# Four pairs' q and k rows set side by side by GpSimd and transposed as 96x128; the output's transposing DMA put ahead of q's and k's

## Chip, core and metric

One core of a Trainium2 chip runs the whole program. The metric is the device time of one execution in microseconds (us), and the kernel is compared with itself before the change. The profile of one execution gives the durations used below.

## What is computed

Attention with a bias that depends on the distance of two positions alone, and behind it two matrix products with a leaky ReLU between them:

```python
scores = (1 / np.sqrt(D)) * np.matmul(q, k.transpose(0, 1, 3, 2))   # B, H, S, D = 8, 8, 576, 64
scores = scores + bias_table[bucket].transpose(2, 0, 1)[None]       # bucket: from |i - j|
attn = softmax(scores)                                              # over the last axis
x = np.matmul(attn, v).transpose(0, 2, 1, 3).reshape(B * S, H * D)  # 4608 x 512
h = x @ w_in                                                        # 512 x 2048
return np.maximum(0.01 * h, h) @ w_out                              # 2048 x 512
```

## The kernel before

**Pairs and bodies.** The heads of a batch are taken two by two: pair `n` is batch `n // 4`, heads `2p` and `2p + 1` with `p = n % 4`, and there are 32 pairs, 0 to 31. Body `n` of the main loop computes the scores of pair `n` (`score`, `qk_mm`, `exp`), multiplies the probabilities of pair `n - 1` with v (`av_tails`, `av` or `av_phase`, `divide`), and makes q and k of pair `n + 1` ready (`transpose_q`, `transpose_k`). From body 4 on, pieces of the two big products fill TensorE in between: `ffn_in` (`pm` from `xT` and `w_in_sb`, L459, its leaky ReLU on ScalarE at L472) and `ffn_out` (L486). From body 8 on, most bodies run in halves of the rows (`body_in_halves`, L407 and L610). The order on each engine is the order in which the program writes the instructions; nothing reorders them.

**q and k.** They are loaded by GpSimd's DMAs with 96 rows on the partitions and six chunks of 64 numbers per head (`qn`, `kn`, two buffers by batch). TensorE needs them transposed. For pairs 0 to 8, `turned_pair` makes, for each of q and k, 12 transposes on TensorE (L275): one for each of six chunks and two heads, 96x64 in, 64x96 out, the two heads' outputs one above the other in `ps_t`. VectorE or ScalarE then copies `ps_t` into `qt` (L290) or `kt` (L294). For pairs 9 to 31 (`by_dma`), VectorE sets the rows of the two heads side by side (`pair_rows`, `pr`, L257), one transposing DMA on SyncE turns q and k at once (`turn_by_dma`, `tu`, L265), and the copies read `tu`. `pr` has four buffers.

**The bias.** After the exponential (L325 and others on ScalarE), `band` multiplies parts of the probabilities `at` by a table `hk` on VectorE (L348, both inputs in SBUF); there are five such products per pair.

**The output.** `divide` writes the quotients of pair `n` into `opair` (L381, L383). They are transposed into `xT`, on TensorE with a copy (`ps_tx`, L433 and L434) or, for pairs 6 and 8 to 30 (`x_by_dma`), by a transposing DMA on SyncE (L423). `ffn_in` of the next 512 tokens can start once the last pair of a batch stands in `xT`.

**SyncE's queue.** In a body in halves, SyncE runs two `fence` instructions (L391, each waits for TensorE and releases a later product), then the turning DMA of q and k, then that of the output, then stores of the output.

**GpSimd's queue.** `loads(n)` issues the DMAs of later batches at the start of body `n`: in body 0 the first half of `w_in`, v of batch 1, the second half of `w_in` and the first half of `w_out`; in body 2 half of q and k of batch 2 and the second half of `w_out`; from body 5 on, each behind a copy of one number (`tick`, L772) that waits for `opair`.

**PSUM.** The tag `m` has two banks, taken in turn by `ps_t`, `ps_tx` and the `pm` of the pieces.

Of the kernel before, what the change touches and what calls it, by code (L numbers as in the profile page):

```python
# [37 lines left out]
def kernel(  # L38
# [10 lines left out]
    nc = tc.nc  # L49
# [7 lines left out]
    n_pairs = H // 2  # L57
# [25 lines left out]
    ident = per.tile([P, P], BF16, name="ident")  # L83
# [11 lines left out]
    RQ = 96  # L95
    NC = S // RQ
    qn = [per.tile([P, H, NC, D], BF16, name=f"qn{i}") for i in range(NBUF)]
    kn = [per.tile([P, H, NC, D], BF16, name=f"kn{i}") for i in range(NBUF)]
# [18 lines left out]
    def load_v_part(b, chunks, h0=0, h1=H):  # L117
        for c in chunks:
            nc.gpsimd.dma_start(  # L119
                out=vn[b % NBUF][:, c, h0:h1, 0:D],  # L120
                in_=v[b, h0:h1, c * P : (c + 1) * P, :].rearrange("h s d -> s h d"),
            )
# [56 lines left out]
    for j, (u, lo, w, m) in enumerate(groups):  # L179
        copy = nc.scalar.copy if j % 3 == 2 else nc.vector.tensor_copy  # L180
        copy(out=ub[:, C0 + lo : C0 + lo + m * w].rearrange("h (m w) -> h m w", w=w),
             in_=e8[:, u : u + m].unsqueeze(2).to_broadcast([H, m, w]))
    row = ub[:, :]
    nc.vector.tensor_copy(
        out=ub[:, C0 - BAND + 1 : C0],
        in_=bass.AP(tensor=row.tensor, offset=row.offset + C0 + BAND - 1,
                    ap=[list(row.ap[0]), [-1, BAND - 1]]),
# [45 lines left out]
    def load_w_in(half):  # L233
        o = slice(half * (DF // 2), (half + 1) * (DF // 2))
        nc.gpsimd.dma_start(out=w_in_sb[:, :, o], in_=moe_w_in[:, o].rearrange("(c p) f -> p c f", p=P))

    def load_w_out(half):
        n = n_fc // 2
        nc.gpsimd.dma_start(
            out=w_out_sb[:, half * n : (half + 1) * n, :],  # L240
            in_=moe_w_out[half * n * P : (half + 1) * n * P, :].rearrange("(f p) e -> p f e", p=P),
        )
# [7 lines left out]
    prs, turned = {}, {}  # L250

    def pair_rows(n):

        b, p = items[n]
        t = prs[n] = pr_pool.tile([RQ, 2, NC, 2 * D], BF16, name="pr")
        for j, src in enumerate((qn, kn)):
            nc.vector.tensor_copy(out=t[:, j, :, :].rearrange("r c (e d) -> r c e d", e=2),  # L257
                                  in_=src[b % NBUF][0:RQ, 2 * p : 2 * p + 2, :, :].rearrange("r e c d -> r c e d"))

    def by_dma(n):  # L260
        return n > 2 * n_pairs
# [5 lines left out]
    def turned_pair(n, j):  # L267

        if by_dma(n):
            return turned[n][:, j * NC : (j + 1) * NC, :].rearrange("p c r -> p r c")  # L270
        ps = ps_m_pool.tile([P, 8 * P], BF16, name="ps_t", tag="m")
        b, p = items[n]
        for c in range(NC):
            for e in range(2):
                nc.tensor.transpose(ps[e * D : (e + 1) * D, c * RQ : (c + 1) * RQ],  # L275
                                    in_=(qn, kn)[j][b % NBUF][0:RQ, 2 * p + e, c, :],
                                    identity=ident[0:RQ, 0:RQ])
        return ps[:, 0:S].rearrange("p (c r) -> p r c", c=NC)
# [13 lines left out]
    def transpose_k(n):  # L292
        kt = kts[n] = kts_[n % 2]
        nc.vector.tensor_copy(out=kt[:, 0:S].rearrange("p (r c) -> p r c", c=NC), in_=turned_pair(n, 1))  # L294
        apart(kt)
# [56 lines left out]
    def av_tails(n):  # L352

        b, p = items[n]
        at4 = at4_[n % 2]
        ops_[n] = op_pool.tile([P, NJ + 1, 2 * D], BF16, name="opair")
        ps = outs[n] = [ps_o_pool.tile([P, 512], FP32, name="ps_o", tag=f"o{e}") for e in range(2)]
        for ic in range(NJ + 1):
            for e in range(2):
                r = slice(e * SL, (e + 1) * SL)  # L360
                nc.tensor.matmul(ps[e][:, ic * (D + 1) : (ic + 1) * (D + 1)],  # L361
                                 lhsT=at4[r, ic * P : (ic + 1) * P], rhs=v4[b % NBUF][r, p, :],
                                 start=(ic == 0), stop=False)
# [25 lines left out]
    def fence(sooner):  # L389

        f = nc.sync.nop(nofuse=True)  # L391
        tc.add_manual_dep(f.ins, sooner.ins.name, ended, reason="behind the last products of these rows")
        return f
# [21 lines left out]
    def x_by_dma(n):  # L415
        return n_pairs + 2 <= n < N - 1 and n != 2 * n_pairs - 1

    def x_transposes(n, spare=None):
        b, p = items[n]
        opair = ops_[n]  # L420
        w = (NJ + 1) * P
        if x_by_dma(n):
            nc.sync.dma_start_transpose(  # L423
                out=xT[p][:, b * S : b * S + w].rearrange("p (i t) -> p i t", t=P),
                in_=opair.rearrange("p i d -> p (i d)"),
            )
            return
        if spare is None:
            ps = ps_m_pool.tile([P, 8 * P], BF16, name="ps_tx", tag="m")
        else:  # L430
            ps = ps_o_pool.tile([P, 8 * P], BF16, name="ps_tx", tag=spare)
        for ic in range(NJ + 1):
            nc.tensor.transpose(ps[:, ic * P : (ic + 1) * P], in_=opair[:, ic, :], identity=ident)  # L433
        nc.vector.tensor_copy(out=xT[p][:, b * S : (b + 1) * S], in_=ps[:, 0:S])  # L434
# [194 lines left out]
    def body_in_halves(n, kinds):  # L629

        loads(n)
        turns = rows_ahead(n) if by_dma(n + 1) else []
        score(n, 0)
        av_tails(n - 1)
        last = fence(av_phase(n - 1, 0))
        score(n, 1)
        T, s = made["out"], at_piece["out"]
        if kinds[0] == "out":
            one, two = open_piece("out", (T, s)), open_piece("out", (T, s + 4))
        else:  # L640
            one, two = open_piece("in"), open_piece("out")
        phase = side_by_side(one, two)
        phase(0, 0, 1)
        av_phase(n - 1, 1, last)
        if n + 1 < N:
            transpose_q(n + 1)
        band(n, 0)
        divide(n - 1, range(2))
        last = fence(phase(0, 1, n_cc))
        score(n, 2)  # L650
        score(n, 3)
        phase(1, 0, n_cc, last)
        band(n, 1)
        if n + 1 < N:
            transpose_k(n + 1)
        score(n, 4)
        if kinds[0] == "in":
            one[2]()
        for m in turns:
            turn_by_dma(m)  # L660
        if x_by_dma(n - 1):
            x_transposes(n - 1)
        while stores:
            o, y = stores.pop(0)
            nc.sync.dma_start(out=o, in_=y)
        if not x_by_dma(n - 1):
            late = [n - 1]
        else:
            late = []
        band(n, 2)  # L670
        if kinds[0] == "out":
            outs_pm[T] = one[0]
            ffn_out(T, s + 1)
            band(n, 4)
            score(n, 5)
            band(n, 5)
            ffn_out(T, s + 2)
            ffn_out(T, s + 3)
            for m in late:
                x_transposes(m, "o0")  # L680
                finished(m)
            outs_pm[T] = two[0]
            for part in range(5, 8):
                ffn_out(T, s + part)
            at_piece["out"] = (s + 8) % n_fc
            made["out"] += at_piece["out"] == 0
            return
        piece_out()
        band(n, 4)
        score(n, 5)  # L690
        band(n, 5)
        piece_out()
        piece_out()
        for m in late:
            x_transposes(m, "o1")
            finished(m)
        room["left"] -= 5
        moe(room["left"], 0)
# [59 lines left out]
    def loads(n):  # L758

        b, p = items[n]  # L760
        if n == 0:
            load_w_in(0)
            load_v_part(1, range(NJ))
            load_v_tail(1)
            load_w_in(1)
            load_w_out(0)
        elif n == 2:
            load_qk(2, 0, H // 2)
            load_w_out(1)
        if b < 1 or p < 1 or b > B - 2:  # L770
            return
        nc.gpsimd.tensor_copy(out=tick, in_=ops_[n - 2][0:1, 0, 0:1])  # L772
        if p == 1:
            load_qk(b + 1, H // 2, H)
            load_v_part(b + 1, (0,))
        elif p == 2:
            load_v_part(b + 1, (1, 2, 3))
        else:
            load_v_tail(b + 1)
            if b + 2 < B:  # L780
                load_qk(b + 2, 0, H // 2)
# [6 lines left out]
    def rows_ahead(n):  # L788
        ms = [m for m in range(n + 2, min(n + AHEAD + 1, N))
              if by_dma(m) and m - (AHEAD if m > 2 * n_pairs + 2 else 2) == n]  # L790
        for m in ms:
            pair_rows(m)
        return ms
# [5 lines left out]
    def score(n, u):  # L799
        exp(n, u, qk_mm(n, u))  # L800
# [44 lines left out]
    n = n_pairs  # L845
# [129 lines left out]
```

## Time and profile before

| | |
|---|---|
| time, median of three runs | 377.12 us (376.32 to 378.21) |
| profiled execution | 375.74 us, its span 374.0 us |
| granted TensorE clock, mean | 0.997 |
| TensorE busy | 362.5 us, 97% of the span |
| ScalarE, VectorE, GpSimd busy | 240.8, 196.5 and 77.3 us |

The page gives one execution: busy time of each engine, the chain of work that ended last, and the costliest groups of instructions by source line. The timeline gives instructions in order with their start, duration and the idle time of the engine before them; a run of equal instructions stands in one row with its count. `PE` is TensorE, `PEld` its weight load, `DVE` VectorE, `ACT` ScalarE, `POOL` GpSimd, `SP` SyncE. The end of a product on TensorE is modelled, so its rows overlap, and the distance from one start to the next is the sharper measure.

### The profile page before, as it was taken

The page shows a single profiled execution, that of the slowest core. Times are in us where ns is not written, and L with a number is a line of the kernel's source. Part 1 is how long each engine was busy: PE and PEld are TensorE (multiplying, and loading weights), DVE is VectorE, ACT ScalarE, POOL GpSimd, SP SyncE. Part 2 cuts the span into 40 slices and gives each one's busy share as a digit, 9 for nine tenths or more (in the row PEclk, how much of TensorE's full clock was granted, in tenths as well). Part 3 has the DMA queues.
Part 4 walks back from the last instruction along what each step waited for, and adds up shares of the span by engine and source line. Part 5 has one row for each costly group of instructions (what it writes and reads, how often), then busy time and mean ns, then how long its engine had stood idle before and what let it go on. Part 6 is the DMA issues. An engine that isn't in the chain of part 4 may idle for free.

```text
span 374.0 us, 10606 instructions
## 1 busy us (share of the span) xinstructions
PE 362.5 (97%) x4516; PEld 187.5 (50%) x4516; DVE 196.5 (53%) x504; ACT 240.8 (64%) x374; POOL 77.3 (21%) x118
## 2 busy tenths in 40 slices
PE   7889999999999999999999999999999999999995
PEld 3455555555555555555555554555555544444442
DVE  3688577776757566666755565665554200100121
ACT  4998887568947787777877776777777364054000
POOL 8773331333023303331233023100000000000000
PEclk9999999999999999999999999999999999999998
DMA  8999999799579979996999599433121000200221
GB/s 103 189 201 184 206 201 158 124 166 169 67 107 163 121 124 122 148 140 121 96 121 145 83 115 156 93 80 71 34 43 47 30 28 0 86 28 0 86 79 64
DMA packets 104360, 40.19 MB, mean 107 GB/s; under 512 B 83184, under 2 KB 98808, under 8 KB 104312
## 3 DMA queue, kind: packets, MB, share of 16 engines
q0 software_dynamic: 53696, 18.36, 47.3%
q1 hardware_dynamic: 50472, 21.02, 28.3%
q8 instruction: 35, 0.57, 0.6%
q10 hardware_dynamic: 144, 0.13, 0.1%
q14 instruction: 13, 0.11, 0.1%
HBM read 37.68 MB, written 9.45 MB: 126 GB/s over the span
## 4 chain that ended last, share of the span: by engine, by line
PE 89%; ACT 4%; DVE 4%; DMA 2%; issue 1%; DVEq 0%; ACTq 0%
PE pm L486 28%; PE pm L459 28%; PE pm L610 8%; PE ps_s L312 7%; PE ps_o L407 6%; PE ps_o L372 4%; DMA xT<-opair 2%; ACT at L325 2%; PE ps_s L315 2%; PE ps_o L361 1%; PE ps_w L750 1%; DVE opair L383 1%; PE ps_t L275 1%; PE ps_tx L433 1%; PE ps_q L305 1%; DVE at L348 1%
## 5 line engine op out<-in xcount | busy, mean ns | idle before, releaser
L325 ACT ACTIVATE at<-ps_s 128x1024 bf16<-128x1024 f32 x128 | 124.5, 1027 | 26.1 <-PE ps_s L312 26.0
L472 ACT ACTIVATE gt<-pm 128x512 bf16<-128x512 f32 x138 | 82.8, 605 | 71.0 <-PE pm L459 70.5
L459 PE MATMUL pm<-xT,w_in_sb 128*128 128x512 bf16 x508 | 118.1, 379 | 0.1
L486 PE MATMUL pm<-w_out_sb,gt 128*128 128x512 bf16 x492 | 113.9, 379 | 0.0
L348 DVE TENSOR_TENSOR at<-at,hk 128x768 bf16<-128x768 bf16 (+3 forms) x160 | 71.0, 454 | 59.3 <-ACT at L325 34.8
L459 PEld LDWEIGHTS <-w_in_sb 128*128 128x128 bf16 x508 | 47.6, 98 | 54.8 <-issue 0.7
L486 PEld LDWEIGHTS <-gt 128*128 128x128 bf16 x492 | 45.0, 98 | 51.4
L504 DVE COPY y<-pm 128x512 f32<-128x512 f32 x35 | 24.2, 692 | 74.8 <-PE pm L486 74.8
L312 PE MATMUL ps_s<-qt,kt 64*128 64x512 bf16 x256 | 43.2, 380 | 3.4 <-ACT at L325 3.0
L610 PE MATMUL pm<-w_out_sb,gt 64*128 64x512 bf16 x168 | 42.2, 376 | 0.0
L610 PE MATMUL pm<-xT,w_in_sb 64*128 64x512 bf16 x136 | 37.7, 376 | 0.9 <-DMA xT<-opair 0.9
L772 POOL COPY tick<-opair 1x1 bf16<-1x1 bf16 x18 | 3.9, 215 | 134.8 <-DVE opair L383 134.8
L119 POOL DMA_DIRECT2D vn<-in_v_dram x32 | 29.9, 940 | 8.8 <-DMA w_out_sb<-in_moe_w_out_dram 3.8
L383 DVE TENSOR_TENSOR opair<-ps_o,rcp 128x320 bf16<-128x320 f32 x64 | 29.7, 488 | 1.6
L407 PE MATMUL ps_o<-vn,at 64*128 64x65 bf16 x1520 | 29.5, 190 | 0.0
L407 PEld LDWEIGHTS <-at 64*128 64x128 bf16 x1520 | 27.1, 94 | 4.4 <-SPq L391 3.0
L312 PEld LDWEIGHTS <-kt 64*128 64x128 bf16 x256 | 11.6, 94 | 25.3 <-issue 16.5
L332 ACT ACTIVATE at<-ps_s 128x576 bf16<-128x576 f32 x32 | 21.8, 680 | 0.2 <-PE ps_s L316 0.2
L381 DVE RECIPROCAL rcp<-ps_o 128x5 f32<-128x5 f32 x64 | 10.0, 182 | 22.3 <-PE ps_o L372 19.3
L328 ACT ACTIVATE at<-ps_q 128x256 bf16<-128x256 f32 x64 | 21.3, 394 | 0.3 <-PE ps_q L305 0.2
L372 PE MATMUL ps_o<-vn,at 128*128 128x65 bf16 x520 | 20.1, 194 | 0.0
L372 PEld LDWEIGHTS <-at 128*128 128x128 bf16 x520 | 17.9, 97 | 3.5 <-issue 0.7
(62 smaller groups left out, 244.4 us busy)
## 6 DMA issues: line engine op xcount, KB each, us to landing
out_dram<-y SPq DMA_DIRECT2D x35, 256.0 KB, 2.2
qn<-in_q_dram POOLq DMA_DIRECT2D x14, 288.0 KB, 5.9
kn<-in_k_dram POOLq DMA_DIRECT2D x14, 288.0 KB, 7.5
vn<-in_v_dram POOLq DMA_DIRECT2D x28, 128.0 KB, 6.4
w_in_sb<-in_moe_w_in_dram POOLq DMA_DIRECT2D x2, 1024.0 KB, 12.4
w_out_sb<-in_moe_w_out_dram POOLq DMA_DIRECT2D x2, 1024.0 KB, 15.9
qn<-in_q_dram POOLq DMA_DIRECT2D x4, 144.0 KB, 4.7
kn<-in_k_dram POOLq DMA_DIRECT2D x4, 144.0 KB, 5.0
```

What stands on the lines that cost most here:

```text
L119: nc.gpsimd.dma_start(out=vn[b % NBUF][:, c, h0:h1, 0:D], in_=v[b, h0:h1, c * P : (c + 1) * P, :].rearrange("h s d -> s h d"),)
L312: nc.tensor.matmul(ps[:, e, :], lhsT=kt[r, u * P : (u + 1) * P], rhs=qt[r, 0:512], start=True, stop=True)
L325: nc.scalar.activation(at[:, :, u, 0:512], ps, AF.Exp, scale=scale)
L348: nc.vector.tensor_tensor(out=o, in0=o, in1=m, op=ALU.mult)
L372: nc.tensor.matmul(ps[:, ic, :], lhsT=at[:, o : o + P], rhs=vn[b % NBUF][:, c, 2 * p + e, :], start=False, stop=(ic == NJ and c == NJ - 1))
L383: nc.vector.tensor_tensor(out=opair[:, :, e * D : (e + 1) * D], in0=ps[:, :, 0:D], in1=rcp.to_broadcast([P, NJ + 1, D]), op=ALU.mult)
L407: m = nc.tensor.matmul(outs[n][e][:, ic * (D + 1) : (ic + 1) * (D + 1)], lhsT=at[halves[r], o : o + P], rhs=vn[b % NBUF][halves[r], c, 2 * ...
L459: nc.tensor.matmul(pm, lhsT=w_in_sb[:, c, f * P : (f + 1) * P], rhs=xT[c][:, t0 : t0 + TT], start=(c == 0), stop=(c == n_cc - 1))
L472: nc.scalar.activation(g, pm, AF.Prelu, bias=0.0, scale=1.0, alpha=0.01)
L486: nc.tensor.matmul(pm, lhsT=gt[:, f, ts * P : (ts + 1) * P], rhs=w_out_sb[:, f, :], start=(f == 0), stop=(f == n_fc - 1))
L504: nc.vector.tensor_copy(out=y, in_=pm)
L610: m = nc.tensor.matmul(pm, lhsT=w[halves[r]], rhs=x[halves[r]], start=(k == 0 and c == 0), stop=(low is not None and k == 1 and c == n_cc ...
```

## The change

For pairs 5 to 8, GpSimd copies the two heads' rows side by side into `pr` (k first, then q, 96x768 each), and TensorE transposes both heads of a chunk at once: six transposes 96x128 for each of q and k in place of twelve 96x64. The copies of pairs 5 and 6 stand in GpSimd's queue in body 0, ahead of the first half of `w_out`; those of pair 7 in body 2 behind the second half of `w_out`; those of pair 8 in body 6 behind three loads of v. For the pairs from 9 on, VectorE still makes the copies, now k ahead of q. In bodies in halves the output's transposing DMA is issued ahead of the one of q and k, where it was behind it. Order and number of the instructions of ScalarE, and the number of those of VectorE and SyncE, stay as they are.

```diff
         t = prs[n] = pr_pool.tile([RQ, 2, NC, 2 * D], BF16, name="pr")
-        for j, src in enumerate((qn, kn)):
-            nc.vector.tensor_copy(out=t[:, j, :, :].rearrange("r c (e d) -> r c e d", e=2),
+        eng = nc.vector if by_dma(n) else nc.gpsimd
+        for j, src in reversed(list(enumerate((qn, kn)))):
+            eng.tensor_copy(out=t[:, j, :, :].rearrange("r c (e d) -> r c e d", e=2),
                                   in_=src[b % NBUF][0:RQ, 2 * p : 2 * p + 2, :, :].rearrange("r e c d -> r c e d"))
...
         for c in range(NC):
+            if n > n_pairs:
+                nc.tensor.transpose(ps[:, c * RQ : (c + 1) * RQ], in_=prs[n][:, j, c, :],
+                                    identity=ident[0:RQ, 0:RQ])
+                continue
             for e in range(2):
...
         if kinds[0] == "in":
             one[2]()
+        late = [n - 1]
+        if x_by_dma(n - 1):
+            x_transposes(late.pop())
         for m in turns:
             turn_by_dma(m)
-        if x_by_dma(n - 1):
-            x_transposes(n - 1)
         while stores:
             o, y = stores.pop(0)
             nc.sync.dma_start(out=o, in_=y)
-        if not x_by_dma(n - 1):
-            late = [n - 1]
-        else:
-            late = []
...
             load_w_in(1)
+            pair_rows(n_pairs + 1)
+            pair_rows(n_pairs + 2)
             load_w_out(0)
         elif n == 2:
             load_qk(2, 0, H // 2)
             load_w_out(1)
+            pair_rows(n_pairs + 3)
...
             load_v_part(b + 1, (1, 2, 3))
+            if b == 1:
+                pair_rows(2 * n_pairs)
```

## The prediction

> **What bounds the kernel now.** I read the page first, then a table of busy time by stretch, then TensorE's waits, then the timeline of the bodies that the change touches.
>
> ```profile
> span 374.0 us, 10606 instructions
> PE 362.5 (97%) x4516; PEld 187.5 (50%) x4516; DVE 196.5 (53%) x504; ACT 240.8 (64%) x374; POOL 77.3 (21%) x118
> ```
>
> TensorE is the bound of the whole, but a share over the span hides where it is not. The table by stretch has, for each, its length and then the busy time of PE, PEld, DVE, ACT and POOL. The first row is body 3 and the start of body 4, the next two are bodies 5 and 6, the last holds body 24 and the start of body 25.
>
> ```profile
> 25.00:33.00 8.00, 7.09 (x151) 4.84 (x148) 6.02 (x18) 7.94 (x12) 3.62 (x5) 1.00 1.61 189
> 38.70:47.40 8.70, 8.70 (x120) 5.05 (x120) 5.33 (x13) 7.14 (x11) 2.83 (x5) 1.00 1.25 204
> 47.40:56.10 8.70, 8.70 (x120) 5.04 (x121) 6.45 (x16) 7.15 (x11) 2.59 (x5) 1.00 1.39 200
> 210.00:230.00 20.00, 19.14 (x296) 10.07 (x295) 11.46 (x29) 14.30 (x22) 5.25 (x8) 1.00 0.87 113
> ```
>
> From 25 to 33 us ScalarE is the bound (7.94 of 8.00 busy), with TensorE and VectorE passing work round in a ring. In bodies 5 and 6 TensorE is busy without a break, so what is taken from it there counts, unless it only waited inside its modelled busy time. In the last row TensorE stands still for 0.86 us, and its list of waits (total, times, longest) names why:
>
> ```profile
> PE pm L610 <- DMA xT<-opair: 0.9, 1, 0.9
> ```
>
> **Part 1: the transposes on TensorE.** The change takes 48 products away: four pairs, q and k, six each. These are body 6's rows, then those of the end of body 7.
>
> ```profile
> 48.78 0.45 PE L275 MATMUL ps_t<-ident,qn 96*64 96x96 bf16 x12
> 49.16 1.04 PE L459 MATMUL pm<-xT,w_in_sb 128*128 128x512 bf16 x4
> 50.74 0.45 PE L275 MATMUL ps_t<-ident,kn 96*64 96x96 bf16 x12
> 51.12 0.61 PE L312 MATMUL ps_s<-qt,kt 64*128 64x512 bf16 x4
> ...
> 51.84 0.45 PE L433 MATMUL ps_tx<-ident,opair 128*128 128x128 bf16 x5
> 52.28 1.89 PE L459 MATMUL pm<-xT,w_in_sb 128*128 128x512 bf16 x8
> 54.01 0.38 PE L315 MATMUL ps_s<-qt,kt 128*128 128x512 bf16 x1
> ...
> 54.25 1.89 PE L459 MATMUL pm<-xT,w_in_sb 128*128 128x512 bf16 x8
> 56.08 0.60 PE L312 MATMUL ps_s<-qt,kt 64*128 64x512 bf16 x4
> ...
> 59.42 0.45 PE L275 MATMUL ps_t<-ident,kn 96*64 96x96 bf16 x12
> 59.80 1.04 PE L459 MATMUL pm<-xT,w_in_sb 128*128 128x512 bf16 x4
> ```
>
> From start to start a side's 12 transposes hold TensorE for 0.38 us. There is a second cost in them. Eight L459 products take 1.73 us when a product with the same 128*128 weights follows (52.28 to 54.01), and 1.83 when one with 64*128 weights follows (54.25 to 56.08): a change of the weights' shape costs 0.10. The old transposes (96*64) stand between 128*128 products, so q pays it on the way in, outside the 0.38, and on the way out, inside. New ones are 96*128; I take them to share a shape class with 128*128, as nothing in the table is nearer. Their price comes from the output's transposes in body 4, and the group of those transposes' weight loads (busy us, mean ns):
>
> ```profile
> 33.57 0.45 PE L433 MATMUL ps_tx<-ident,opair 128*128 128x128 bf16 x5
> 33.86 0.38 PE L315 MATMUL ps_s<-qt,kt 128*128 128x512 bf16 x1
> ```
>
> ```profile
> L433 PEld LDWEIGHTS <-opair 128*128 128x128 bf16 x40 | 2.3, 97 | 2.6 <-DVE opair L383 2.2
> ```
>
> Five transposes with 128 weight columns and 128 moving columns take 0.29 us, 58 ns each. Six take 0.35 at that price, or 0.26 if the 96 moving columns scale it. So a q side gains 0.38 + 0.10 less 0.26 to 0.35: 0.13 to 0.22; I take 0.20. Against this speaks a rule of the Trainium skill, TensorE: Matmul & The Clock Gate, section "LDWEIGHTS (loading the stationary operand)": the load takes its columns divided by 1.2 ns, so that twice the columns take twice as long. By it, as an estimate, six loads of 107 ns would hold TensorE for 0.64 us and a side would lose 0.16 where I let it gain 0.20; the 58 ns above, with 128 columns each, do not bear that out for loads in a row.
>
> Not every side counts. On the k sides of bodies 5 and 6 the gain runs into a wait: at 51.84 five transposes take 0.44 where they took 0.29, since the next `pm` needs the bank that VectorE is still emptying of `ps_t`:
>
> ```profile
> 51.48 0.75 DVE L294 COPY kt<-ps_t 128x576 bf16<-128x576 bf16 x1
> ```
>
> It ends at 52.23, and TensorE goes on at 52.28. That copy is behind `divide` on VectorE, released by the end of `av` before the k transposes, so shorter transposes there only lengthen the wait: 0. In body 4 both sides run into waits for VectorE and ScalarE (the q side into the leaky ReLU of the piece before): 0. On the k side of body 7 a 128*128 product follows (59.80) and no such wait is seen: 0.20. Sum: three q sides and one k side, 0.8 us (0.5 to 0.9).
>
> **Part 2: the output's DMA first.** The chain of waits has, before that stop of TensorE:
>
> ```profile
> 215.16 0.89 DVE opair L383 x2
> ...
> 217.13 8.64 DMA xT<-opair
> ```
>
> and SyncE's timeline what it did meanwhile:
>
> ```profile
> 215.59 1.44 SPq L265 DMA_TRANSPOSE tu<-pr  x1
> ```
>
> `opair` is there at 216.05, but SyncE was busy issuing the other DMA until 217.03. First in the queue, the output's goes out 1.1 us earlier, and no transfer of q and k is ahead of it. 1.1 is more than the 0.86 that TensorE lost, so the whole stop goes: 0.86 (0 if the landing does not move with the issue). What is late next is nothing on DMA: the turned q and k, now some 1.9 us later, are read two bodies on, and a body is 8.7 us at its shortest. Behind both in SyncE's queue are stores and the next body's fences, which wait 0.5 us longer at most, with half a body to spare. VectorE's k-ahead-of-q order costs nothing, since one DMA waits for both.
>
> **Part 3: GpSimd's copies.** Eight copies of 96x768. No row has such a copy; the nearest are fills of a constant and of the identity, and the selection that finishes it; VectorE's own copy of that size (group row: busy us, mean ns) stands beside them.
>
> ```profile
> 0.24 0.10 POOL L959 MEMSET const-float32-0.0<- 128x1 f32 x1 [0.24 <-issue]
> 2.69 0.24 POOL masks.py:197 MEMSET ident<- 128x128 bf16 x1
> 3.01 0.29 POOL masks.py:199 TENSOR_SCALAR_AFFINE_SELECT ident<-ident 128x128 bf16<-128x128 bf16 x1
> ```
>
> ```profile
> L257 DVE COPY pr<-kn 96x768 bf16<-96x768 bf16 x23 | 8.1, 350 | 0.0
> ```
>
> From 1 to 128 elements a fill grows by 0.14 us, 1.14 ns per element, so 768 elements take 0.1 + 0.87: about 1.0 us. As ends I keep VectorE's 0.35 and, from the selection's 1.5 ns per element, 1.25. GpSimd's queue around them:
>
> ```profile
> 26.92 0.80 POOL L235 DMA_DIRECT2D w_in_sb<-in_moe_w_in_dram  x1
> 31.72 0.90 POOL L239 DMA_DIRECT2D w_out_sb<-in_moe_w_out_dram  x1 [4.00 <-DMA w_in_sb<-in_moe_w_in_dram]
> ...
> 54.03 0.62 POOL L132 DMA_DIRECT2D v<-in_v_dram  x1 [3.13 <-DMA w_out_sb<-in_moe_w_out_dram]
> ```
>
> Four copies stand in a hole of 4.0 us. Behind them are queued `w_out`, q, k and v of batch 2 and the ticks. Even 2 us of lateness there is covered: issues wait for earlier transfers (the 4.00 and 3.13), and the second `w_out` half, landed by 54, is first read by products behind the last row of body 7 above (59.80). The copies of pairs 5 and 6 end by 33 even if they wait as reckoned below, and pair 6's are read from body 5 on, behind 38.70. If that cover were gone, TensorE would wait microsecond for microsecond.
>
> The price lies on VectorE. A copy of one number on GpSimd shows it:
>
> ```profile
> 36.73 0.65 DVE L348 TENSOR_TENSOR at<-at,hk 128x192 bf16<-128x192 bf16 x2
> 36.90 0.52 POOL L772 COPY tick<-opair 1x1 bf16<-1x1 bf16 x1
> 41.05 0.18 POOL L772 COPY tick<-opair 1x1 bf16<-1x1 bf16 x1 [1.45 <-DVE opair L383]
> ```
>
> It takes 0.18, but 0.52 when a band product runs, and ends 0.04 after that product (37.42 against 37.38): GpSimd waited for VectorE's whole instruction. No row shows the other direction; whatever both need whole, I take to be needed by both alike, so that a band that finds a copy running waits for its end. The Trainium skill, SBUF — State Buffer, section "Who interferes with whom", says so too: a VectorE instruction with two SBUF inputs and a GpSimd one that reads SBUF exclude each other, and the later is blocked until the earlier ends. The trace agrees for the one direction, with the 0.52 us above. The bands beside the copies are, before the change:
>
> ```profile
> 27.94 0.42 DVE L348 TENSOR_TENSOR at<-at,hk 128x512 bf16<-128x512 bf16 x1
> ...
> 28.98 0.55 DVE L348 TENSOR_TENSOR at<-at,hk 128x768 bf16<-128x768 bf16 x1
> ...
> 29.98 1.11 DVE L348 TENSOR_TENSOR at<-at,hk 128x768 bf16<-128x768 bf16 x3
> ```
>
> If copies and bands take turns: the first copy runs from 27.72 to 28.72, the band of 27.94 starts at 28.72 (0.78 late) and ends at 29.14; the second copy runs to 30.14, the next band, due at 29.76, to 30.69; the third copy to 31.69, and the three bands of 29.98 start then, 1.7 late. TensorE reads what they write:
>
> ```profile
> 30.32 0.67 PE L361 MATMUL ps_o<-v,at 64*128 64x65 bf16 x10
> 30.92 0.78 PE L372 MATMUL ps_o<-vn,at 128*128 128x65 bf16 x20
> ```
>
> These products start as the bands end (the last at 31.09), so they come 1.7 late, and body 4 is a ring of waits with no slack: **1.7 lost**. Below zero nothing is possible, since these copies relieve no engine in this stretch; with copies of 0.35 the bands are held up by some 0.2 us, with 1.25 by 2.5. Pair 7's two copies fall ahead of body 5, where VectorE is busy for 5.33 of 8.70 us, pair 8's near body 6's bands: 0 taken, for pair 8 up to 0.8 (most of one copy) kept for the range.
>
> **Sum.** -0.8 - 0.86 + 1.7 = 0.0 against the profiled execution: 375.74 stays 375.8. The median of the runs is 377.12, 1.4 above that execution, and moves alike: 377.2 us.
>
> **The rivals.** *GpSimd keeps the port (slower).* If a queued copy starts before the one ahead has let go, VectorE's band of 27.94 waits for all four, to 31.72: 3.8 late. Then -1.66 + 3.8 = +2.1: 379.3. It decides from a loss of 3.6 us in bodies 3 and 4 (1.9 and the gains); for it speaks that the four have no wait between them, against it that VectorE's request is older than the third and fourth copy. *VectorE is not held up (faster).* Only the gains stay: -1.66, 375.5, or 375.3 with the transposes' gain at its upper end. For it: only GpSimd is seen waiting; against: it waited for the whole instruction, as for something exclusive. *The new transposes cost more than the old*, because weight loads of 128 columns do not overlap here: six at the 97 ns of the group row are 0.58 us for a side, which then loses 0.10 where it was to gain 0.20; four sides make +1.2 and 378.4, with turns taken on VectorE. It is the cited rule's case; the 58 ns of five such transposes in a row speak against it.
>
> **How the numbers follow.** A measurement of this kernel tells about 0.5% from no change, 1.9 us: below 375.2 is faster, above 379.0 slower. The three runs before lie 1.9 us apart, so each case has a spread of some 0.5 us about its value. Taking turns, 0.34: 0.23 within 0.5%, 0.06 faster (short copies), 0.05 slower (copies of 1.25 us and pair 8's 0.8). GpSimd keeping the port, 0.29: 0.23 slower, 0.06 within. VectorE not held up, 0.33: 0.19 faster, 0.14 within. Dearer transposes, 0.04, within. Together faster 0.25, same 0.47, slower 0.28. The range goes from 374.7 (gains alone at their upper end, less the spread) to 379.8 (the slower rival and the spread).
>
> **What would show it.** Right: L275 in two shapes, a new q side of some 0.28 us between 128*128 products; no wait for `xT` in body 25; GpSimd's copies near 1 us; in body 3 a band that starts as a copy ends. Wrong: bands at their old distances beside running copies, or the first band behind all four copies; an `xT` that lands as late as before; transposes that wait for `pr`, or `w_out` pieces that wait for their load.

## The result, and the profile after

| | before | after |
|---|---|---|
| median of 20 runs each | 376.24 us (374.81 to 381.56) | 378.72 us (377.12 to 380.13) |
| profiled execution | 375.74 us, span 374.0 | 377.12 us, span 375.3 |
| granted clock, mean | 0.997 | 0.992 |

The ratio is 1.0067, with an interval from 1.0053 to 1.0082: 0.67% slower, 2.5 us. One run of before, 381.56 us, lies over 1.5% above the fastest and does not enter the ratio. The profiled execution of after is the quickest of its 20, so its trace shows less than the median lost; two more traces of the same kernel stand among the experiments.

The page's head of after (span; busy us, share and count of each engine) beside the first lines of the prediction:

```profile
span 375.3 us, 10456 instructions
PE 358.1 (95%) x4425; PEld 187.9 (50%) x4468; DVE 199.9 (53%) x504; ACT 241.1 (64%) x374; POOL 83.3 (22%) x126
```

TensorE has 48 products fewer by the weight loads (4516 before, 4468 now; some matmul records are missing), GpSimd eight instructions more. VectorE has as many instructions as before and is busy for 3.4 us longer: it did no more work, it stood within its instructions. Two places make up nearly all of it. One is the band of 27.98 below. The other is a pair of bands beside pair 7's copies, which take 1.96 us where two such bands took 0.65 before (the row of 36.73 in the prediction):

```profile
39.71 1.96 DVE L353 TENSOR_TENSOR at<-at,hk 128x192 bf16<-128x192 bf16 x2
```

The table by stretch (length, then busy time of PE, PEld, DVE, ACT, POOL, granted clock, DMA share, GB/s) says where TensorE lost by it. First the stretches of the prediction, bodies 5 and 6 and the end of body 24:

```profile
38.70:47.40 8.70, 8.44 (x109) 4.91 (x105) 7.06 (x15) 6.95 (x11) 5.86 (x9) 1.00 1.24 206
47.40:56.10 8.70, 8.56 (x104) 4.95 (x106) 6.61 (x16) 7.46 (x13) 4.10 (x6) 1.00 1.40 201
210.00:230.00 20.00, 19.68 (x299) 10.50 (x300) 11.77 (x31) 14.86 (x26) 4.03 (x7) 1.00 0.72 115
```

TensorE has no stop for `xT` in the last row. The loss is earlier. The same view of bodies 3 and 4, before and then after:

```profile
28.00:31.20 3.20, 3.02 (x60) 1.81 (x57) 2.98 (x9) 3.14 (x6) 0.00 (x0) 1.00 1.56 191
31.20:34.60 3.40, 3.24 (x62) 2.22 (x59) 2.42 (x7) 3.25 (x5) 2.01 (x3) 1.00 2.40 162
```

```profile
28.00:31.20 3.20, 1.07 (x26) 0.64 (x22) 3.17 (x5) 1.95 (x3) 3.20 (x5) 0.99 1.51 191
31.20:34.60 3.40, 3.37 (x47) 2.43 (x47) 2.01 (x5) 2.23 (x4) 1.49 (x3) 0.51 2.28 162
```

After the change TensorE is busy for a third of the first row, where it was busy for 3.02 of 3.20 us, while VectorE and GpSimd are both "busy" throughout; in the second row it is busy throughout, at a granted clock of 0.51 where it was 1.00. The timeline of VectorE and GpSimd (start, duration) shows the cause:

```profile
27.98 2.57 DVE L353 TENSOR_TENSOR at<-at,hk 128x512 bf16<-128x512 bf16 x1
30.47 0.18 DVE L386 RECIPROCAL rcp<-ps_o 128x5 f32<-128x5 f32 x1
30.68 0.49 DVE L388 TENSOR_TENSOR opair<-ps_o,rcp 128x320 bf16<-128x320 f32 x1
31.09 0.55 DVE L353 TENSOR_TENSOR at<-at,hk 128x768 bf16<-128x768 bf16 x1
```

```profile
27.84 0.75 POOL L235 DMA_DIRECT2D w_in_sb<-in_moe_w_in_dram  x1 [0.19 <-issue]
28.58 0.84 POOL L258 COPY pr<-kn 96x768 bf16<-96x768 bf16 x1
29.35 0.82 POOL L258 COPY pr<-qn 96x768 bf16<-96x768 bf16 x1
30.12 1.10 POOL L258 COPY pr<-kn 96x768 bf16<-96x768 bf16 x1
31.18 1.14 POOL L258 COPY pr<-qn 96x768 bf16<-96x768 bf16 x1
```

The band that took 0.42 us takes 2.57. It ends at 30.55, so its own 0.42 us cannot have begun before 30.13; the second copy ends at 30.17. So it stood through the first two copies. Then the sides take turns: the third and fourth copies take 1.10 and 1.14 where an undisturbed one takes 0.82 to 0.84. The band holds up what is queued behind it on VectorE, `rcp` and `opair`, and TensorE waits for those; the first of its waits (total, times, longest) from 25 to 60 us is

```profile
PE ps_tx L438 <- DVE opair L388: 2.2, 1, 2.2
...
```

Before the change there was no such wait. The half clock follows directly behind this stop.

To set traces side by side I use the start of a body's first product of v's tail (`av_tails`, L366 in after), less the same start before the change. What a row gains or loses from one column to the next was lost or gained in that body. This is my own subtraction of start times from the traces, in us:

```
                     body 3  body 4  body 5  body 6  body 7  body 8  body 25  body 26
after                 +0.04   +2.60   +2.98   +2.76   +2.54   +2.10   +2.10    +1.06
changed, second look  +0.17   +2.81   +3.78   +3.55   +3.33   +2.88   +2.88    +1.84
changed, third look   -0.42   -0.42   +3.97   +3.75   +3.53   +3.08   +3.08    +2.04
x_behind              +0.58   +3.39   +5.76   +5.54   +5.32   +4.88   +4.88    +4.96
spaced                +0.07   +0.07   +5.92   +5.70   +5.48   +5.03   +5.03    +3.99
warm                  +0.39   +2.29   +3.65   +3.43   +3.45   +3.01   +3.01    +1.97
late                  +0.68   +0.69   +0.69   +1.25   +4.43   +3.98   +4.04    +3.00
fill                  +1.22   +1.22   +1.21   +0.98   +0.76   +0.31   +1.47    +0.43
no_copy               +2.43   +2.44   +2.42   +2.20   +1.98   +1.53   +1.53    +0.49
x_first               +0.46   +0.46   +0.46   +0.47   +0.46   +0.46   +0.47    -0.57
by_vector             +0.67   +0.67   +0.67   +0.45   +0.64   +0.72   +0.71    -0.32
```

The first column differs from trace to trace, also in kernels that are the same up to there: in `no_copy` TensorE waits for bands whose table `hk` landed late (VectorE's wait: 4.05 us), and runs at a granted clock of 0.50 from 21.49 to 24.90. The distances behind it are what the kernels differ in. For after they are +2.94 in bodies 3 and 4, -0.22, -0.22 and -0.44 in bodies 5 to 7 (the new transposes), -1.04 in body 25 (the output's DMA): +1.06, and another 0.29 at the very end, against 1.3 by the spans.

### The profile page after: what moved, and what is told of

Same layout as the page of the kernel before. It is cut to its first block, busy times and chain, and to the rows that moved or that the text cites. A ratio compares the mean times of both kernels' runs of the same rounds, so it can differ in the third digit from the quotient of the medians.

```text
span 375.3 us, 10456 instructions
## 1 busy us (share of the span) xinstructions
PE 358.1 (95%) x4425; PEld 187.9 (50%) x4468; DVE 199.9 (53%) x504; ACT 241.1 (64%) x374; POOL 83.3 (22%) x126
## 4 chain that ended last, share of the span: by engine, by line
PE 88%; DVE 4%; DMA 3%; ACT 2%; issue 2%; SPq 0%; DVEq 0%; ACTq 0%
PE pm L491 28%; PE pm L464 28%; PE pm L615 9%; PE ps_s L317 8%; PE ps_o L412 6%; PE ps_o L377 4%; DMA hk<-u_row 2%; PE ps_s L320 2%; DVE at L353 1%; PE ps_o L366 1%; ACT at L330 1%; PE ps_q L310 1%; DVE opair L388 1%; PE ps_tx L438 1%; DMA u_row<-ub 1%
## 5 line engine op out<-in xcount | busy, mean ns | idle before, releaser
L491 PE MATMUL pm<-w_out_sb,gt 128*128 128x512 bf16 x468 | 109.3, 379 | 3.3 <-issue 3.0
L353 DVE TENSOR_TENSOR at<-at,hk 128x768 bf16<-128x768 bf16 (+3 forms) x160 | 74.7, 475 | 57.8 <-ACT at L330 33.7
```

Source lines behind the costliest of these rows:

```text
L353: nc.vector.tensor_tensor(out=o, in0=o, in1=m, op=ALU.mult)
L491: nc.tensor.matmul(pm, lhsT=gt[:, f, ts * P : (ts + 1) * P], rhs=w_out_sb[:, f, :], start=(f == 0), stop=(f == n_fc - 1))
```

## The experiments

Each names its edit against before or against the changed kernel. Ratios are to the kernel before on the same chip, whose median was 376.34 us beside `x_first`, `x_behind`, `no_copy` and `late`, and 376.04 beside `fill`, `spaced`, `warm` and `by_vector`. They are not quotients of these medians, which for `x_first` and `no_copy` would give 0.9973 and 0.9984; each is to be read with its interval.

**The output's DMA alone (`x_first`).** Before, with this edit only:

```diff
+        late = [n - 1]
+        if x_by_dma(n - 1):
+            x_transposes(late.pop())
         for m in turns:
             turn_by_dma(m)
-        if x_by_dma(n - 1):
-            x_transposes(n - 1)
...
```

> The kernel before with one part of the change: in bodies in halves the output's transposing DMA goes ahead of the one of q and k; transposes and copies as before. Theory (the prediction's part 2): the stop of 0.86 us for xT in body 25 goes, the span falls from 374.0 to 373.1, the time by 0.2%. Rival: executions without the profiler do not have that stop, or the transfer lands as late as before; then the ratio to before is 1.000 within 0.1%.

Measured: 375.33 us, ratio 0.9966 (0.9943 to 0.9989). In its trace the wait for `xT` is gone, and body 25 is 1.04 us shorter (0.47 to -0.57). The part is a gain by itself, 0.2 us more than the stop that the profile showed. TensorE's products at the stop, before and here:

```profile
224.57 0.37 PE L610 MATMUL pm<-xT,w_in_sb 64*128 64x512 bf16 x1
225.81 0.37 PE L610 MATMUL pm<-xT,w_in_sb 64*128 64x512 bf16 x1 [0.86 <-DMA xT<-opair]
```

```profile
225.03 0.37 PE L610 MATMUL pm<-xT,w_in_sb 64*128 64x512 bf16 x1
225.25 0.37 PE L610 MATMUL pm<-xT,w_in_sb 64*128 64x512 bf16 x1
```

From start to start it is 1.24 us before and 0.22 here, so 1.02 of the 1.04 us were lost at this one place. The list of waits counts 0.86 because it starts from the modelled end of the product ahead (224.57 and 0.37), while undisturbed products start 0.22 apart. The output's DMA in the queue of SyncE in after, now first:

```profile
218.17 1.21 SPq L428 DMA_TRANSPOSE xT<-opair  x1
219.44 2.57 SPq L266 DMA_TRANSPOSE tu<-pr  x1
```

**The change without that part (`x_behind`).** After, with the two DMAs in the old order:

```diff
-        late = [n - 1]
-        if x_by_dma(n - 1):
-            x_transposes(late.pop())
         for m in turns:
             turn_by_dma(m)
+        if x_by_dma(n - 1):
+            x_transposes(n - 1)
...
```

> The changed kernel with the output's transposing DMA behind the one of q and k again. Theory: the stop for xT in body 25 comes back, 0.86 us over the changed kernel, a ratio of 1.009 to before. Rival: the order is worth nothing, the ratio stays near 1.0067.

Measured: 379.43 us, 1.0087 (1.0061 to 1.0113), and the old wait is back in the list of its waits behind 200 us:

```profile
PE pm L615 <- DMA xT<-opair: 0.9, 1, 0.9
```

The copies cost more in this trace than in that of after, 5.18 us over bodies 3 and 4 (0.58 to 5.76), though nothing differs up to there. So the price differs between executions.

**The transposes without copies (`no_copy`).** After, with the four `pair_rows` calls on GpSimd left out and the new transposes reading 96x128 of `qn` and `kn`, two neighbouring chunks of one head; so pairs 5 to 8 work on other numbers than theirs:

```diff
...
-                nc.tensor.transpose(ps[:, c * RQ : (c + 1) * RQ], in_=prs[n][:, j, c, :],
+                d = min(c, NC - 2)
+                nc.tensor.transpose(ps[:, c * RQ : (c + 1) * RQ],
+                                    in_=(qn, kn)[j][b % NBUF][0:RQ, 2 * p, d : d + 2, :].rearrange("r c d -> r (c d)"),
...
```

> The changed kernel without GpSimd's eight copies: the transposes of pairs 5 to 8 are 96x128 too, but read two neighbouring chunks of one head from the loaded rows, so q and k of these pairs are other numbers; all else is computed. Theory (GpSimd's copies hold up VectorE's band in body 3, TensorE stops for 2.2 us and then runs at half clock): no stop, clock 1.00 throughout, span near 374.0 - 0.9 - 0.86 = 372.3, ratio to before near 0.995. Rival (the new transposes are dearer, or something else in the change costs): the ratio stays above 1.000 and rows of the transposes show it.

Measured: 375.73 us, 0.9973 (0.9947 to 0.9998); the expected 0.995 lies within the interval. No band of bodies 3 and 4 is late and they cost nothing (2.43 to 2.42); bodies 5 to 7 gain 0.22, 0.22 and 0.45, body 25 1.04. So the loss hangs on the copies, and the new transposes keep their gain without them. By the medians the copies cost 3.0 us (378.72 less 375.73).

**Fills for copies (`fill`).** After, with a fill of the same 96x768 piece of `pr` in place of each copy, so that pairs 5 to 8 have zeros for q and k. The fill writes SBUF and reads nothing:

```diff
+            if not by_dma(n):
+                eng.memset(t[:, j, :, :].rearrange("r c (e d) -> r c e d", e=2), 0.0)
+                continue
```

> The changed kernel with GpSimd's eight copies replaced by fills of the same tiles with zero, so q and k of pairs 5 to 8 are zero; all else is computed. Theory 1 (the band and the copy exclude each other because both read SBUF): fills hold up no band, every band keeps its length of before, TensorE's stop in body 3 stays under 0.3 us, body 4 starts no later than body 3 did. Theory 2 (any long instruction of GpSimd holds VectorE up): bands are stretched as beside the copies, the stop stays near 2 us.

Measured: 375.3 us, 0.9986 (0.9961 to 1.0011). The bands beside the four fills (timeline of VectorE, then of GpSimd) have their old length:

```profile
30.20 0.55 DVE L356 TENSOR_TENSOR at<-at,hk 128x768 bf16<-128x768 bf16 x1
...
31.20 1.12 DVE L356 TENSOR_TENSOR at<-at,hk 128x768 bf16<-128x768 bf16 x3
```

```profile
30.14 2.80 POOL L259 MEMSET pr<- 96x768 bf16 x4
```

Bodies 3 and 4 lose nothing (1.22 to 1.21). In the whole trace no band is more than 0.04 us longer than the usual one of its shape. (This trace loses 1.2 us between bodies 8 and 25, which I did not follow up; no fill runs there.) GpSimd was as busy in the same place, wrote the same bytes, and no band noticed. So neither its being busy nor its writing holds VectorE up; a copy, which also reads SBUF, does. That is the rule of the Trainium skill, SBUF — State Buffer, section "Who interferes with whom": a VectorE instruction with two SBUF inputs contends with a GpSimd one that reads SBUF, not with one that only writes. Both halves agree with what is seen here: a band of 128x768 takes 0.55 us beside fills, and up to 3.24 beside copies (the third look, below). That it is the reading, and nothing else in which a copy differs from a fill, no run here tells apart.

**A fill behind each copy (`spaced`).** After, with a fill of a scratch tile behind each of the eight copies. It asks whether a band waits for one copy or for a row of them:

```diff
+            if not by_dma(n):
+                eng.memset(pause, 0.0)
```

> The changed kernel with a fill of a scratch tile (128x768, written by GpSimd and read by nobody) behind each of GpSimd's eight copies. Theory 1 (a queued copy takes the port before the one ahead has let go, so that the band of body 3 waits for two): with a fill between them the band waits for one copy at most, about 0.8 us where it waited 2.1; TensorE's stop in body 3 shrinks from 2.2 us to about 1 and its clock stays at 1.00. Theory 2 (the band waits for whatever GpSimd does): copies and fills make it wait longer than 2.1 us, and TensorE's stop grows beyond 2.2.

Measured: 379.89 us, 1.0091 (1.0061 to 1.0122). The two timelines, VectorE's and GpSimd's:

```profile
29.05 1.79 DVE L356 TENSOR_TENSOR at<-at,hk 128x768 bf16<-128x768 bf16 x1
...
31.12 2.69 DVE L356 TENSOR_TENSOR at<-at,hk 128x768 bf16<-128x768 bf16 x3
```

```profile
29.57 0.84 POOL L259 COPY pr<-kn 96x768 bf16<-96x768 bf16 x1
30.34 0.75 POOL L262 MEMSET pause<- 128x768 bf16 x1
31.02 0.83 POOL L259 COPY pr<-qn 96x768 bf16<-96x768 bf16 x1
31.79 0.74 POOL L262 MEMSET pause<- 128x768 bf16 x1
32.47 0.82 POOL L259 COPY pr<-kn 96x768 bf16<-96x768 bf16 x1
```

Each band now ends within one copy and its own length: the first at 30.84, 0.43 us behind the copy's end at 30.41, where it takes 0.55 alone. With a fill between two copies no band waits for a second copy. But the copies are spread over twice the time and meet three bands in a row in place of one, and the sum is no smaller: 5.85 us over bodies 3 and 4. TensorE's stop did not shrink to the expected 1 us: it is 2.6 us long, and the granted clock behind it is 0.50 for 6.8 us, which is part of the 5.85. Splitting the row of copies up was no remedy.

**TensorE kept busy in its stop (`warm`).** After, with ten products on unused data ahead of the output's transposes of body 3, to take the half clock away:

```diff
+            if n == 3:
+                pw = ps_m_pool.tile([P, 512], FP32, name="ps_w", tag="m")
+                for _ in range(10):
+                    nc.tensor.matmul(pw, lhsT=junk[:, 0:P], rhs=junk, start=True, stop=True)
```

> The changed kernel with ten products of a tile of zeros (128x512, about 2.2 us at full clock) on TensorE ahead of body 3's output transposes, where it stood still for 2.16 us. Theory (of the 2.9 us that bodies 3 and 4 lose, about 2.1 are the stop and 0.9 the half clock behind it): the granted clock stays at 1.00 behind the stop and body 5 starts about 0.9 us earlier than in the changed kernel, 2.1 us behind the kernel before. Rival (the clock costs nothing, since ScalarE sets the pace there): body 5 starts as late as in the changed kernel.

Measured: 378.39 us, 1.0056 (1.0034 to 1.0077). In its trace the stretch that ran at 0.51 runs at full clock:

```profile
31.20:34.60 3.40, 3.17 (x58) 1.99 (x57) 2.69 (x7) 2.42 (x5) 2.53 (x4) 1.00 2.26 166
```

From the output's transposes of body 3 to the k transposes of body 4, TensorE needs 4.78 us in after (31.23 to 36.01), 4.01 here (31.42 to 35.43) and 3.88 before (29.12 to 33.00). So the half clock is worth some 0.8 us in after, as an estimate from these starts. The start of body 4 is no measure of it: in this trace the first band is only 0.34 us longer (0.76 for 0.42), `opair` is written by 29.72, and it is the ten products themselves that keep TensorE until 31.42. Over bodies 3 and 4 this trace loses 3.26 us (0.39 to 3.65), no less than after, since the next bands meet copies, pair 7's too (a wait of 1.1 for `qt`). The medians of the two kernels lie 0.3 us apart, less than the intervals tell. The half clock adds to the loss; that it is not its cause is shown by the third look below, which loses more at a clock of 1.00.

**Copies later (`late`).** After, with pair 5 turned in the old way and the copies of pairs 6 and 7 behind the second half of `w_out`; pair 8's stay:

```diff
...
-            pair_rows(n_pairs + 1)
-            pair_rows(n_pairs + 2)
...
             load_w_out(1)
+            pair_rows(n_pairs + 2)
             pair_rows(n_pairs + 3)
```

> The changed kernel with pair 5 transposed as before, and the copies of pairs 6 and 7 put behind the second half of w_out in GpSimd's queue, near 37 us, where VectorE is idle between body 4's last bands and body 5; pair 8 as in the change. Theory (a copy costs only where a band that TensorE waits for meets it): the stop in body 3 is gone, the three pairs keep their 0.9 us, ratio near 0.995. Rival (copies cost wherever they run, by about 3 us for eight): six of them give a ratio near 1.001.

Measured: 376.41 us, 1.0001 (0.9969 to 1.0032); the gain that was to be left did not come. The interval does not exclude the rival's 1.001; the trace tells more, though its execution, 379.01 us, is the slowest of the 12 (374.69 to 379.01). Bodies 3 and 4 lose nothing now, but its waits from 25 to 60 us have two new ones:

```profile
PE ps_q L310 <- DVE opair L388: 1.7, 1, 1.7
...
PE ps_t L276 <- POOL pr L258: 0.6, 1, 0.6
```

0.6 us is pair 6, whose copies come too late. 1.7 is pair 8, whose two copies, at 51.80 and 52.57, meet a band that waits through both:

```profile
51.52 2.16 DVE L353 TENSOR_TENSOR at<-at,hk 128x512 bf16<-128x512 bf16 x1
```

Body 6 loses 3.2 us by that (1.25 to 4.43): the stop, and a granted clock of 0.50 behind it from 55.84 to 59.25. In after the same two copies run at 51.1 and 51.9, where no band runs, and cost nothing. So where they fall against the bands decides between nothing and 3.2.

**VectorE copies (`by_vector`).** After, with all rows copied by VectorE, pairs 6 to 8 in places where it idles, and pair 5 turned in the old way:

```diff
-        eng = nc.vector if by_dma(n) else nc.gpsimd
+        eng = nc.vector
...
     band(n, 4)
+    pair_rows(n + 2)
     moe(1)
...
```

> The changed kernel with no copies on GpSimd: VectorE sets the rows of pairs 6, 7 and 8 side by side at the end of bodies 4, 5 and 6 (two copies of 0.35 us each), pair 5 is transposed as before; the output's DMA stays first. Theory (the order of DMAs is worth 1.0 us, the transposes 0.9, and only the copies on GpSimd cost): no long stop in bodies 3 to 7, the gain of the transposes less at most 0.3 us per body that VectorE is later; ratio 0.994 to 0.996. Rival (VectorE is late for the divisions of bodies 5 to 7): the ratio is that of the DMA order alone, 0.9966, or above.

Measured: 375.0 us, 0.9968 (0.9947 to 0.9989), the shortest span of all, 373.2 us. But it is not told apart from the DMA order alone (0.9966): what the transposes gain goes back into a new wait,

```profile
PE ps_t L276 <- DVE pr L258: 0.6, 2, 0.4
```

and bodies 5 to 7 come out at +0.05. Both versions beat before and after; the DMA's place is what they have in common.

**Two more looks at the changed kernel (`again_1`, `again_2`).** No edit: a second and a third trace, since the first was of the quickest execution.

> The changed kernel once more, for a second and a third trace. Theory: what the copies cost varies with where they fall against the bands; the gains do not vary. Expected: the loss from the start of body 3 to that of body 6 between 2.5 and 5.5 us, more than the 2.7 of the first trace since its execution was the quickest of 20; -0.22, -0.22, -0.44 at bodies 6 to 8 and -1.0 at body 26 as before. Rival: the loss in bodies 3 to 5 is the same 2.7 to 3.0 each time, and the slower executions lose their time in the first three bodies, where loads are late.

> As for the run before it: copies' loss different from trace to trace, by the theory; the same loss and a different start, by the rival.

Measured: 377.92 and 378.19 us. Bodies 3 and 4 lose 3.61 and 4.39 us where the first trace lost 2.94, and the rest is as it was: the theory, not the rival. The third trace loses its 4.39 us at a granted clock of 1.00 from 25 to 47 us. The second look, VectorE's band and GpSimd's copies:

```profile
28.11 2.96 DVE L353 TENSOR_TENSOR at<-at,hk 128x512 bf16<-128x512 bf16 x1
```

```profile
28.38 0.89 POOL L258 COPY pr<-kn 96x768 bf16<-96x768 bf16 x1
29.15 0.88 POOL L258 COPY pr<-qn 96x768 bf16<-96x768 bf16 x1
29.92 0.87 POOL L258 COPY pr<-kn 96x768 bf16<-96x768 bf16 x1
30.69 1.07 POOL L258 COPY pr<-qn 96x768 bf16<-96x768 bf16 x1
```

The band ends at 31.07: it stood through three copies. In the third look the first band had ended, and the next one met the copies:

```profile
28.55 3.24 DVE L353 TENSOR_TENSOR at<-at,hk 128x768 bf16<-128x768 bf16 x1
```

```profile
28.25 0.84 POOL L258 COPY pr<-kn 96x768 bf16<-96x768 bf16 x1
29.02 0.82 POOL L258 COPY pr<-qn 96x768 bf16<-96x768 bf16 x1
29.79 0.82 POOL L258 COPY pr<-kn 96x768 bf16<-96x768 bf16 x1
30.56 0.82 POOL L258 COPY pr<-qn 96x768 bf16<-96x768 bf16 x1
...
38.11 0.84 POOL L258 COPY pr<-kn 96x768 bf16<-96x768 bf16 x1
38.87 0.83 POOL L258 COPY pr<-qn 96x768 bf16<-96x768 bf16 x1
```

It ends at 31.79, 0.41 behind the end of the fourth copy at 31.38: it stood through all four, and none of them was any longer for it. Pair 7's two then held a band as well, and TensorE waited 2.4 us for the first and 1.7 for `qt` behind the second:

```profile
PE ps_o L366 <- DVE at L353: 2.4, 1, 2.4
PE pm L464 <- DVE qt L295: 1.7, 1, 1.7
```

## Why the prediction was right or wrong, point by point

377.2 us was given as likeliest, no change from the median shown; the median came out at 378.72, 0.67% above that of before over as many runs. It lies in the range, between the likeliest case and the slower rival (379.3), but the change is on the slower side of the 0.5%, where the likeliest case had none. That 377.2 is only 1.5 us off is in part luck: it was counted from 377.12, the median of three runs, and that of 20 is 376.24, so that the change forecast was 0.0 and the one measured 2.5 us. The signs of all three parts were right; one of them was too small.

- *Transposes, -0.8.* Measured -0.88 in after, and -0.88 to -0.90 in six other traces in which all four pairs have the new form; in the seventh, `warm`, pair 8's copies hold up a band (0.85 us for 0.26), and 0.64 is left. In after a q side is six products in 0.25 us, here from 59.92 to 60.17 (timeline of TensorE):

```profile
59.92 0.42 PE L276 MATMUL ps_t<-ident,pr 96*128 96x96 bf16 x6
60.17 1.03 PE L464 MATMUL pm<-xT,w_in_sb 128*128 128x512 bf16 x3
...
61.65 0.42 PE L276 MATMUL ps_t<-ident,pr 96*128 96x96 bf16 x6
61.91 1.03 PE L464 MATMUL pm<-xT,w_in_sb 128*128 128x512 bf16 x4
```

 That is 0.25 and 0.26 us a side, the lower end of the 0.26 to 0.35 expected, and 42 to 43 ns a product. The four sides that were to count did, at 0.22 each: one in body 5, one in body 6, both of body 7. The rival of dearer transposes falls. So does, for loads in a row, the rule that the prediction cited beside it (the Trainium skill, TensorE: Matmul & The Clock Gate, section "LDWEIGHTS (loading the stationary operand)"): 128 columns at its 107 ns a load would, as an estimate, have made 0.64 us of the six.
- *The output's DMA, -0.86.* Measured -1.04, in `x_first` and in after alike. The step was right and 0.2 us short: the stop was read off the list of waits as 0.86, and from start to start it was 1.02, as `x_first` shows. The distance of starts, which the section on the profile before calls the sharper measure, would have given it.
- *GpSimd's copies, +1.7.* This term was mis-sized: 2.9, 3.6 and 4.4 us in three traces of the kernel and 5.2 in `x_behind`, which has the same copies; about 3.0 to 3.4 by the medians (378.72 less those of `no_copy` and `fill`). The length of a copy was taken too long, 1.0 us against 0.82 to 0.84, and that they exclude the bands was right. What failed is "taking turns". A band can wait for several copies that are queued one right behind the other: two in after, three in the second look, four in the third, two for pair 8's in `late`. In the rows of after the first copies overlap, 29.35 against 29.42, as the rival "GpSimd keeps the port" supposed; that this is the reason is not shown. The rival is nearer to the mechanism, with its four copies in one trace, and its +2.1 was closest to the +2.5 measured; but in after and in the second look a band did come in between two queued copies, so it is no rule either. The reason held against it, that VectorE's request is older than the third and fourth copy, is refuted by the third look, where the band's row starts before those of three of the four copies. `spaced` is the check from the other side: with a fill between the copies a band waits for one. Of the signs that were named, both kinds came: a band that begins as a copy ends (30.13 and 30.17 in after, by the length of the band), and a band behind all four copies (the third look).
- *The clock.* Not in the sum at all. Behind a stop of 2.2 us TensorE ran at half clock for 3.4 us in after, worth some 0.8 by the estimate under `warm`.
- *Pairs 7 and 8, 0.* They cost 0.4 us or less in after, and up to 1.7 in another execution of the same kernel. "Up to 0.8 for pair 8" was too small a bound, as `late` shows with 3.2, the half clock included.

The cover that was named held: no piece of `w_out` and no transpose of after waited for its load or for `pr`.

## What to carry to other kernels

A copy on an idle GpSimd is not free where VectorE multiplies two tiles from SBUF: price it at the bands it can meet, each held up for as much as the whole row of queued copies, and look at which product of TensorE stands behind those bands. A gain of 0.2 us per place on the busiest engine does not pay for one such stop. Where two transfers of one queue are ready together, put the one that is waited for sooner first: here that was the whole gain that any version kept which computes all pairs from their own numbers.

## What the hardware showed that was not expected

- A waiting VectorE instruction with two inputs in SBUF need not come between GpSimd copies that follow each other without a gap: bands of 0.42, 0.42 and 0.55 us took 2.57, 2.96 and 3.24, through two, three and four copies. What lets it in earlier in one trace than in another is not settled.
- A band can be held before the copy's row begins. In after the band of 27.98 would have ended alone at 28.40, and the first copy's row starts at 28.58; until then GpSimd issues a DMA (the row of 27.84). Such an issue alone does not hold a band: in the trace of before I count 43 bands that start beside one, and none is over 0.01 us longer than the usual one of its shape. Either a copy takes hold ahead of its row, or the rows of GpSimd stand too late; no run tells which.
- The clock behind a stop. Four stops of 2.2 to 2.6 us (after, second look, `x_behind`, `spaced`) were followed by a granted clock of 0.50, for 3.4 us in the first two and 6.8 in the others. One of 1.7 us in `late` was too, for 3.4 us, and in `no_copy` the clock went to 0.50 for 3.4 us behind stops of only 0.6 and 0.9 us. One of 2.4 us in the third look was not, and its clock stayed at 1.00. So the length of the stop alone does not decide it. The Trainium skill, TensorE: Matmul & The Clock Gate, section "What's actually happening", puts the step down to half clock behind an idle window of about 3.4 us that runs freely. The lengths of the slow stretches agree with such a window (3.4 and 6.8 us); that the stop need not last one does not.
